# A searched instruction order for two mixer-and-MLP layers on one core: 857 of its 1187 operations reordered

## The chip, the cores and the metric

The kernel runs on one NeuronCore of one Trainium2 chip. The core has five engines with instruction queues of their own: TensorE (PE in the profile; its weight loads are PEld), VectorE (DVE), ScalarE (ACT), GpSimd (POOL) and SyncE (SP), which here issues nearly all the DMAs. The metric is device time in microseconds (us) of one execution; the kernel before took 236.13 us, the median of three runs (235.84 to 236.35).

## The reference

The input q is a sequence of 2048 tokens with 512 channels. Four residual steps follow each other, a mixer A and an MLP B, twice:

```python
x = A_q
x = x + _A_ref(_layernorm(x), A_k, A_v, A_shift_k, A_ssm_k, A_ssm_D)
x = x + _B_ref(_layernorm(x), B_w1, B_b1, B_w2, B_b2)
x = x + _A_ref(_layernorm(x), A_k, A_v, A_shift_k, A_ssm_k, A_ssm_D)
x = x + _B_ref(_layernorm(x), B_w1, B_b1, B_w2, B_b2)
```

A shifts k through a four-tap filter, multiplies it by v, convolves the product along the sequence with a kernel as long as the sequence (`ssm_k`, by FFT in the reference, plus `ssm_D` times the product), and multiplies the result by the normalised x. Since the convolution does not depend on x, its output Y is computed once and used in both layers. B normalises again, multiplies by w1 (512 x 1376), adds b1, takes a gelu, multiplies by w2 (1376 x 512) and adds b2.

## The kernel before

The program records 1187 operations with `P.op`, each with the engines that may run it, a duration used for planning, and what it reads and writes. An operation is one instruction, or a group of matmuls on one accumulator. `arrange` then places them: `SEQ` is a list of operation numbers that gives the global order (each engine's queue is that list cut to its own operations, and runs strictly in it), `ENGS` gives the engine of each operation that could run on more than one, and `BANKS` the PSUM bank of each accumulator. `sync` adds the semaphore waits that the order needs. All three tables were written by a search outside the kernel.

The first part of the program, roughly to 55 us of the span, computes the convolution of the first 1024 tokens as a Fourier transform made of matmuls: `ht`, `h1`, `h2` (transform of the filter), `fir` (the shift and the product with v), `x1`, `x2` (transform of the product), elementwise products, and `i1`, `i2` (inverse). The second 1024 tokens go through the same stages (`h2_1`, `fir4` to `fir7`, `x1_1`, `x2_1`, `i1_1`, `i2_1`) between the MLP work of the first half. Three of their steps use DMAs from one part of the on-chip memory to another or from DRAM: eight `swap` DMAs (L460, `ar<-ar`) exchange even and odd partitions of the filter's transform once `h2_1` (VectorE, L788) is done, and the products `p2` (VectorE, L475 on 128x2048) multiply what they bring; eight transposing loads of k (L800) fill the shift's input.

The layers are worked in 13 blocks of tokens, numbered 0 to 12: of 128 or 256 tokens in the first half (L920's matmuls have 128 or 256 columns there), of 512 in the second. Block n goes through: `q` statistics (VectorE L831, L832; then L836, L838, L846 or L843 on GpSimd or VectorE), the normalisation (ScalarE L856 or VectorE L857), `y` (two products or sums on VectorE, L475), `z` statistics and normalisation the same way, a transposition of the normalised 128x512 tile so that channels lie on partitions, then `m1` (PE L920, eleven groups of four matmuls, each followed by a gelu on ScalarE, L925), `m2` (PE L954, eleven matmuls per 128 tokens) and the residual sum (VectorE L958). The transposition is done by PE in blocks 0 and 1, and by a DMA transpose (L900, issued by SP) in blocks 2 to 12: two or four of them per block, 30 in all. The first matmul group of a block's `m1` needs all its transposes landed. The chain from one layer's `m2` to the next block's `m1` is long, and PE works on other blocks in that time; which, is what the tables decide.

In arrange's planning a DMA lands 2300 ns plus its bytes over 385 per ns after its issue, which is 2640 ns for one DMA transpose of 128 KB.

Of the kernel before, what the change touches and what calls it, by code (L numbers as in the profile page):

```python
# [36 lines left out]
class Prog:  # L37
# [65 lines left out]
            "vpvvvvavvavvvvvavavpvvvaa")  # L103
    BANKS = (
            "26624320240260660466027405640260464422140204626240406006442460424046462002242440224402622420604066466004"
            "64437020665061071760610567714342477554774645676076415011601640607710627426534031026021423236345773476356"
            "05721367332244501304047053300705405345357130760457666515312732321600130735714203533")

    def __init__(self, nc):
# [885 lines left out]
```

## Time and profile before

| what | value |
| --- | --- |
| median of 3 runs (range) | 236.13 us (235.84 to 236.35) |
| the profiled execution's own time | 238.78 us |
| its span, first to last instruction | 237.0 us |
| PE busy | 224.1 us (95%) |
| VectorE busy | 179.1 us (76%) |
| ScalarE busy | 165.8 us (70%) |
| GpSimd busy | 50.0 us (21%) |
| granted TensorE clock | 1.0 throughout |

The profiled execution is 2.65 us longer than the median of the runs. A row of the waits names the waiting engine and line, then who ended the wait. A row of the chain says what the end of the program hung on at that time, in order of time. A row of the timeline gives start, duration, engine, line, and output and input tiles: `ar` is the on-chip array that holds nearly everything in bf16, `sm` the small statistics in fp32, `ps` the PSUM. SPq is SP issuing a DMA, which takes SP's time too; the DMA's landing comes later.

### The profile page before, as it was taken

What the parts mean: (1) busy time and instruction counts of PE and PEld (TensorE: products, weight loads), DVE (VectorE), ACT (ScalarE), POOL (GpSimd) and SP (SyncE); (2) the same over time, 40 slices, a digit from 0 to 9 for tenths busy, and PEclk for the clock granted to TensorE, in tenths of its full rate; (3) what the DMA queues carried; (4) which work ended last, traced back from release to release, by engine and by line L of the source; (5) the groups of instructions that cost most, each with busy time, mean ns of one, the idle gap of its engine ahead of it and who ended that gap; (6) DMA issues with size and microseconds to landing.
All of it is one profiled execution on the core that took longest, in us unless ns stands there. A gap on an engine that the chain in (4) does not pass through costs nothing.

```text
span 237.0 us, 6515 instructions
## 1 busy us (share of the span) xinstructions
PE 224.1 (95%) x2765; PEld 146.0 (62%) x2765; DVE 179.1 (76%) x363; ACT 165.8 (70%) x263; POOL 50.0 (21%) x110
## 2 busy tenths in 40 slices
PE   6888887999989979999999999999999999999995
PEld 3777776967848577667967575744444444444444
DVE  0698999999999899689999987584459779414013
ACT  3788999999948669998997999677047305731730
POOL 2270122007402453244002431303020110200000
PEclk9999999999999999999999999999999999999999
DMA  6999489938949520032500203400400140142002
GB/s 192 375 386 278 155 248 265 313 80 124 181 111 284 98 24 0 4 45 46 173 9 3 47 3 66 111 3 19 116 0 3 22 111 0 22 69 110 23 21 70
DMA packets 40105, 24.93 MB, mean 105 GB/s; under 512 B 23590, under 2 KB 33676, under 8 KB 40076
## 3 DMA queue, kind: packets, MB, share of 16 engines
q1 hardware_dynamic: 39778, 24.36, 38.6%
q8 instruction: 22, 0.36, 0.6%
q10 hardware_dynamic: 298, 0.16, 0.3%
q14 instruction: 7, 0.06, 0.1%
HBM read 13.23 MB, written 2.10 MB: 65 GB/s over the span
## 4 chain that ended last, share of the span: by engine, by line
PE 75%; ACT 8%; DMA 8%; DVE 5%; SPq 1%; issue 1%
PE ps L920 32%; PE ps L954 28%; DMA ar<-ar 6%; ACT ar L480 6%; PE ps L695 4%; PE ps L590 3%; PE ps L578 3%; DMA ar<-in_A_ssm_k_dram 2%; ACT ar L856 2%; DVE ar L475 2%; DVE ar L641 2%; PE ps L717 1%; DVE ar L481 1%; PE ps L635 1%; SPq L460 1%
## 5 line engine op out<-in xcount | busy, mean ns | idle before, releaser
L925 ACT ACTIVATE ar<-ps,sm 128x256 bf16<-128x256 f32 (+4 forms) x143 | 66.1, 521 | 37.2 <-PE ps L920 36.8
L920 PE MATMUL ps<-ar 128*128 128x256 bf16 (+4 forms) x572 | 81.6, 297 | 2.9 <-DMA ar<-ar 2.7
L480 ACT ACTIVATE ar<-ps 128x1024 bf16<-128x1024 f32 (+3 forms) x78 | 72.1, 1003 | 12.1 <-PE ps L578 4.8
L954 PE MATMUL ps<-ar 128*128 128x512 bf16 (+1 forms) x341 | 79.6, 379 | 0.0
L920 PEld LDWEIGHTS ps<-ar 128*128 128x128 bf16 (+1 forms) x572 | 52.6, 100 | 30.2 <-DMA ar<-ar 3.7
L475 DVE TENSOR_TENSOR ar<-ar 128x512 bf16<-128x512 bf16 (+2 forms) x104 | 62.9, 642 | 5.9 <-ACT ar L856 4.4
L954 PEld LDWEIGHTS ps<-ar 128*128 128x128 bf16 (+1 forms) x341 | 32.3, 98 | 35.1 <-ACT ar L925 0.2
L831 DVE BATCH_NORM_STATS2 sm<-ar 128x6 f32<-128x512 bf16 x64 | 42.8, 683 | 0.5
L958 DVE TENSOR_TENSOR ar<-ar,ps 128x512 bf16<-128x512 bf16 x31 | 20.8, 680 | 28.7 <-PE ps L954 28.7
L856 ACT ACTIVATE ar<-ar,sm 128x512 bf16<-128x512 bf16 x39 | 30.7, 811 | 10.2 <-DVE sm L843 10.2
L838 POOL TENSOR_TENSOR sm<-sm 128x2 f32<-128x2 f32 (+2 forms) x26 | 21.4, 824 | 41.4 <-DVE sm L836 39.8
L836 POOL TENSOR_SCALAR sm<-sm 128x2 f32<-128x2 f32 (+2 forms) x19 | 5.9, 310 | 92.0 <-DVE sm L832 91.8
L590 PE MATMUL ps<-ar 128*128 128x64 bf16 x512 | 18.5, 193 | 1.7 <-DVE ar L481 0.6
L578 PE MATMUL ps<-ar 128*64 128x128 bf16 x512 | 18.3, 221 | 1.9 <-ACT ar L480 1.2
L590 PEld LDWEIGHTS ps<-ar 128*128 128x128 bf16 x512 | 16.9, 98 | 4.7 <-DVE ar L481 1.2
L578 PEld LDWEIGHTS ps<-ar 128*64 128x64 bf16 x512 | 15.0, 110 | 5.0 <-ACT ar L480 2.6
L481 DVE CAST ar<-ps 128x1024 bf16<-128x1024 f32 x11 | 13.4, 1216 | 1.5 <-PE ps L578 1.2
L846 POOL TENSOR_SCALAR sm<-sm 128x1 f32<-128x1 f32 x34 | 13.6, 414 | 1.7
L695 PE MATMUL ps<-ar 64*128 64x64 bf16 (+1 forms) x384 | 12.4, 203 | 0.6 <-DVE ar L475 0.4
L695 PEld LDWEIGHTS ps<-ar 64*128 64x128 bf16 (+1 forms) x384 | 11.8, 113 | 1.8 <-ACT ar L480 0.7
L857 DVE TENSOR_SCALAR ar<-ar,sm 128x512 bf16<-128x512 bf16 x25 | 9.8, 413 | 2.5 <-POOL sm L846 2.2
L832 DVE BATCH_NORM_AGGREGATE sm<-sm 128x2 f32<-128x6 f32 x64 | 10.5, 173 | 0.8
(45 smaller groups left out, 93.1 us busy)
## 6 DMA issues: line engine op xcount, KB each, us to landing
ar<-ar SPq DMA_DIRECT2D x16, 256.0 KB, 3.6
ar<-tab_s SPq DMA_DIRECT2D x9, 256.0 KB, 6.4
ar<-in_A_ssm_k_dram SPq DMA_DIRECT2D x8, 256.0 KB, 5.8
ar<-in_A_q_dram SPq DMA_DIRECT2D x8, 256.0 KB, 5.1
ar<-in_A_v_dram SPq DMA_DIRECT2D x8, 256.0 KB, 5.2
out_dram<-ar SPq DMA_DIRECT2D x7, 256.0 KB, 2.5
ar<-in_B_w_dram SPq DMA_DIRECT2D x4, 344.0 KB, 4.6
ar<-in_B_w_dram SPq DMA_DIRECT2D x5, 256.0 KB, 5.2
```

Source lines behind the costliest of these rows:

```text
L475: return P.op(eng, lambda e: e.tensor_tensor(o, a, b, op), dur, reads=[a, b] + list(more), writes=[o])
L480: return e.activation(dst, src(), AF.Copy)
L578: r = e.matmul(Q(tl, 64 * ri, 64, i * 128, [1, 128]), w, m, start=True, stop=True)
L590: r = e.matmul(Q(tl, 0, 128, i // 8 * 512 + i % 8 * 4, [32, 16], [1, 4]), w, m, start=True, stop=True)
L695: r = e.matmul(Q(tl, 0, 128, i, *([32, 16], [1, 4]) if split else ([1, 128],)), w, m, start=n == 0, stop=n == 1)
L831: P.op(DVE, lambda e, sj=sj, x=x: e.bn_stats(sj, x), 600.0, reads=[x], writes=[sj])
L838: P.op(POOL, lambda e: e.tensor_tensor(r, v, hf, ALU.pow), 420.0 + 149.0 * n, reads=[v, hf], writes=[r])
L856: return e.activation(o, x, AF.Identity, bias=u, scale=r)
L920: r = e.matmul(Q(tl, 0, rows, 0, [1, w]), a, m, start=dk == 0, stop=dk == 3)
L925: P.op(ACT, lambda e, dst=dst, tl=tl, rows=rows, bias=bias, w=w: e.activation(dst, Q(tl, 0, rows, 0, [1, w]), AF.Gelu_apprx_tanh, bias=bia ...
L954: r = e.matmul(Q(tl, 0, 128, 0, [1, 512]), ins[fc][0], ins[fc][1], start=fc == 0, stop=fc == 10)
L958: P.op(DVE, lambda e, x=x, tl=tl: e.tensor_tensor(x, x, Q(tl, 0, 128, 0, [1, 512]), ALU.add), 604.0, reads=[x], writes=[x], tile=tl)
```

## The change

The first 330 numbers of `SEQ` stay. The 857 others stand in a new order, found by a search like the one before in which each on-chip DMA transpose had a longer time reserved than the 2640 ns. With the new order, 25 operations run on another engine of those allowed (nine move from ScalarE to VectorE, eight the other way, five from VectorE to GpSimd, three back), and most accumulators of the reordered part are in other banks. The operations themselves, their sizes and the code around the tables are the same, and so are the durations in `arrange`. The first line that differs in `SEQ`, cut:

```diff
-        419, 414, 258, 411, 389, 412, 415, 293, 456, 588, 413, 416, 482, 408, 417, 251, 460, 409, 534, 452, 461, 426,
...
+        419, 414, 482, 411, 389, 448, 415, 258, 292, 456, 449, 466, 534, 457, 454, 483, 467, 412, 486, 455, 452, 588,
...
```

What moves is seen on the engines' queues. On VectorE, around block 2's second statistics: L788 is `h2_1` of the convolution, L475 on 128x512 is `y` of blocks 2 and 3, L831 and L832 are the `z` statistics of block 2. Before:

```order
L788 SCALAR_TENSOR_TENSOR ar<-ar,sm,ps 128x16x32 x6
L475 TENSOR_TENSOR ar<-ar 128x512
L788 SCALAR_TENSOR_TENSOR ar<-ar,sm,ps 128x16x32
L475 TENSOR_TENSOR ar<-ar 128x512
L788 SCALAR_TENSOR_TENSOR ar<-ar,sm,ps 128x16x32
L831 BN_STATS sm<-ar 128x6
L475 TENSOR_TENSOR ar<-ar 128x512
L832 BN_AGGR sm<-sm 128x2
L831 BN_STATS sm<-ar 128x6
L832 BN_AGGR sm<-sm 128x2
L788 SCALAR_TENSOR_TENSOR ar<-ar,sm,ps 128x16x32 x5
```

And now:

```order
L788 SCALAR_TENSOR_TENSOR ar<-ar,sm,ps 128x16x32 x5
L475 TENSOR_TENSOR ar<-ar 128x512
L788 SCALAR_TENSOR_TENSOR ar<-ar,sm,ps 128x16x32
L475 TENSOR_TENSOR ar<-ar 128x512 x2
L831 BN_STATS sm<-ar 128x6 x2
L832 BN_AGGR sm<-sm 128x2 x2
L788 SCALAR_TENSOR_TENSOR ar<-ar,sm,ps 128x16x32 x2
L843 SCALAR_TENSOR_TENSOR sm<-sm 128x2
```

Ahead of block 2's statistics there were eight L788 and now there are six; L843, the negated mean, was on GpSimd (as L846) and is now on VectorE behind two more L788.

On ScalarE, around block 3's second normalisation: the rows of 128x256 and 96x256 are the eleven gelus of block 2; the first two L856 among or behind them normalise block 3's two tiles for their DMA transposes, the next ones are block 4's, and L480 empties an accumulator of `x1_1`. Before:

```order
L925 ACTIVATE ar<-ps,sm 128x256 x7
L925 ACTIVATE ar<-ps,sm 96x256
L925 ACTIVATE ar<-ps,sm 128x256
L856 ACTIVATE ar<-ar,sm 128x512
L925 ACTIVATE ar<-ps,sm 128x256 x2
L856 ACTIVATE ar<-ar,sm 128x512 x2
L480 ACTIVATE ar<-ps 128x1024
L856 ACTIVATE ar<-ar,sm 128x512
```

And now:

```order
L925 ACTIVATE ar<-ps,sm 96x256
L925 ACTIVATE ar<-ps,sm 128x256 x7
L856 ACTIVATE ar<-ar,sm 128x512
L925 ACTIVATE ar<-ps,sm 128x256
L856 ACTIVATE ar<-ar,sm 128x512
L925 ACTIVATE ar<-ps,sm 128x256 x2
L856 ACTIVATE ar<-ar,sm 128x512 x2
L480 ACTIVATE ar<-ps 128x1024
```

The first of the two moved ahead of one gelu, the second ahead of two, and the second of block 4 ahead of the L480.

On SP, in the same place, the queue of DMAs before (L800 loads k, L900 are the DMA transposes of blocks 2 and on, the eight L460 of `ar<-ar` the swaps):

```order
L800 DMA_TRANSPOSE ar<-in_A_k_dram 128x4x128
L900 DMA_TRANSPOSE ar<-ar 128x4x128 x2
L460 DMA ar<-ar 64x8x256 x8
L900 DMA_TRANSPOSE ar<-ar 128x4x128 x8
L460 DMA ar<-in_A_q_dram 128x1024 x4
```

And now:

```order
L900 DMA_TRANSPOSE ar<-ar 128x4x128 x2
L460 DMA ar<-ar 64x8x256 x5
L900 DMA_TRANSPOSE ar<-ar 128x4x128 x4
L460 DMA ar<-ar 64x8x256 x3
L900 DMA_TRANSPOSE ar<-ar 128x4x128 x4
L460 DMA ar<-in_A_q_dram 128x1024 x4
```

Three of the eight swaps now stand behind the four transposes of blocks 3 and 4.

On ScalarE in the stage of `x2_1`: L480 with 128x2x16x32 empties an accumulator of `x2_1`, L925 are gelus of blocks 4 and 5, L856 normalises block 6. Before:

```order
L480 ACTIVATE ar<-ps 128x2x16x32
L856 ACTIVATE ar<-ar,sm 128x512 x2
L480 ACTIVATE ar<-ps 128x2x16x32 x3
L925 ACTIVATE ar<-ps,sm 128x256
L480 ACTIVATE ar<-ps 128x2x16x32 x2
L925 ACTIVATE ar<-ps,sm 128x256
L925 ACTIVATE ar<-ps,sm 96x256
L925 ACTIVATE ar<-ps,sm 128x256 x2
L480 ACTIVATE ar<-ps 128x2x16x32
L925 ACTIVATE ar<-ps,sm 128x256 x11
```

And now:

```order
L480 ACTIVATE ar<-ps 128x2x16x32
L856 ACTIVATE ar<-ar,sm 128x512 x2
L925 ACTIVATE ar<-ps,sm 96x256
L480 ACTIVATE ar<-ps 128x2x16x32 x4
L925 ACTIVATE ar<-ps,sm 128x256 x3
L480 ACTIVATE ar<-ps 128x2x16x32
L925 ACTIVATE ar<-ps,sm 128x256 x15
```

The longest run of these evacuations was three and is now four; the gelus that stood between them now stand before or after.

More of the change, by code (lines that the diff above doesn't have):

```diff
@@ L58 @@
         533, 445, 424, 260, 209, 410, 422, 425, 586, 286, 446, 261, 423, 587, 406, 447, 294, 418, 257, 250, 407, 388,
[41 rows of a table removed]
[41 rows of a table added]
     ENGS = (
             "pvavvvvvavpvpapapaaavaaaaavaavaavavvvppvvvaavvaaavaavvaaaaaaaaavaaaaavaaaavaaaaaaapppvaaaaaaaaaaaaaaaaaa"
-            "aaaaaaaaaaapvapvvavpvppaappvvppaavpaappaappaappaappaappaappavppaappaavpvvppavppaapvaavavvvaaapvvavvvpaav"
-            "vpvvvvavvavvvvvavavpvvvaa")
+            "avaaaaaaaaapvapvvavpvppaappvvpvaavpaappaappaappaappaappavppvappaappaappvappaapvaapvavvavvvvvapvvvvvppvaa"
+            "avvvvaappavvapvavavpvvava")
     BANKS = (
-            "26624320240260660466027405640260464422140204626240406006442460424046462002242440224402622420604066466004"
-            "64437020665061071760610567714342477554774645676076415011601640607710627426534031026021423236345773476356"
-            "05721367332244501304047053300705405345357130760457666515312732321600130735714203533")
+            "26624320240260660466027405640260464422140204626240406006442460424046462022442640460444626002206020640220"
+            "04023022660051677767117660640311026376367637332542537030213654742352762454741476061377362300423726574027"
+            "07315704314621527766215047034261015330227471565340011503350731745320154030276054756")
     def __init__(self, nc):
```

80 rows, old and new, of the table SEQ are left out of this document.

## The prediction

> **What bounds the kernel now.** I read the page's busy times first, then the busy time by stage, then the waits, and last the chain around the waits that PE has. In the table by stage each row gives a stretch, its length, and each engine's busy time in it.
>
> ```profile
> span 237.0 us, 6515 instructions
> PE 224.1 (95%) x2765; PEld 146.0 (62%) x2765; DVE 179.1 (76%) x363; ACT 165.8 (70%) x263; POOL 50.0 (21%) x110
> ...
> 44.00:56.00 12.00, 11.62 (x197) 9.03 (x194) 11.60 (x28) 11.13 (x14) 2.02 (x5) 1.00 0.63 147
> 56.00:71.20 15.20, 13.91 (x286) 10.51 (x284) 15.17 (x31) 11.63 (x31) 5.38 (x14) 1.00 0.72 144
> 71.20:84.30 13.10, 11.49 (x171) 7.87 (x172) 12.41 (x27) 8.52 (x16) 4.18 (x12) 1.00 0.75 175
> 84.30:125.00 40.70, 40.70 (x479) 29.90 (x479) 37.69 (x54) 37.61 (x68) 11.61 (x16) 1.00 0.18 43
> 125.00:153.00 28.00, 27.89 (x404) 18.79 (x404) 24.03 (x68) 24.33 (x38) 9.11 (x18) 1.00 0.22 49
> 153.00:235.00 82.00, 81.54 (x403) 38.58 (x400) 43.57 (x105) 36.20 (x59) 6.40 (x11) 1.00 0.17 41
> ```
>
> PE is the bound. From 84.3 us to 235 us it is busy 150.1 of 150.7 us, and the change alters no matmul: nothing can be won there, only lost. The first 330 operations are kept, which covers the first 44 us. What is left to win lies between 44 and 84.3 us, where PE misses 0.38 + 1.29 + 1.61 = 3.3 us. VectorE misses only 0.40 + 0.03 + 0.69 = 1.1 us there, so it is close behind.
>
> The waits name who ended PE's idle time, with the total, the number of waits and the longest:
>
> ```profile
> PEld ps L920 <- DMA ar<-ar: 3.7, 2, 2.1
> PE ps L920 <- DMA ar<-ar: 2.7, 2, 1.6
> ```
>
> Two waits of `m1` for a DMA transpose hold 2.7 of the 3.3 us. The chain shows both:
>
> ```profile
> 66.84 4.29 DMA ar<-ar
> 71.14 0.05 issue
> 71.19 4.55 PE ps L920 x40
> ...
> 77.67 0.71 ACT ar L856
> 78.38 0.49 SPq L900
> 78.87 0.45 issue
> 79.31 4.88 DMA ar<-ar
> 84.20 0.05 issue
> 84.25 7.60 PE ps L920 x68
> ```
>
> The first is block 2's second transpose: issued at 66.84, landed 4.29 us later. The second is block 3's, which also found SP still busy with the issue before it: its normalisation ended at 78.38, its issue came at 79.31. The timeline gives PE's own wait in each place, in the brackets:
>
> ```profile
> 71.19 4.98 PE L920 MATMUL ps<-ar 128*128 128x256 bf16 x44 [1.06 <-DMA ar<-ar]
> 84.25 1.92 PE L920 MATMUL ps<-ar 128*128 128x256 bf16 x16 [1.61 <-DMA ar<-ar]
> ```
>
> All 30 transposes together took this long to land (least, median, most), and a stretch without other traffic shows what one takes alone:
>
> ```profile
> DMA to landing us min/median/max: 2.4/2.5/4.9
> ...
> ar<-ar SPq DMA_TRANSPOSE x4, 2.5
> ```
>
> So the two that PE waited for, at 4.29 and 4.88 us, were late by 1.8 and 2.4 us against 2.5. The DMA table of the stretch 66.8 to 71.2 has one packet of the instruction queue beside the swaps, and so has 79.3 to 84.3; the undisturbed stretch (186 to 195 us, block 11) has none.
>
> ```profile
> q8 instruction: 1, 0.02, 1.6%
> ...
> q8 instruction: 1, 0.02, 1.1%
> ...
> q8 instruction: 22, 0.36, 0.6%
> ```
>
> [...]
>
> **The change part by part.**
>
> *Block 2's transposes.* Two L788 fewer stand on VectorE ahead of block 2's statistics, and VectorE is never idle there (15.17 of 15.20 us), so the statistics, the normalisations and the transposes behind them come earlier by those two instructions:
>
> ```profile
> 57.52 1.40 DVE L788 SCALAR_TENSOR_TENSOR ar<-ar,sm,ps 128x512 bf16<-128x512 bf16 x2
> ```
>
> That is 1.40 us, more than the 1.06 us wait. PE's work between the same points is the same set of groups in another order. The wait closes even if the transpose is as late as it was: -1.06 us. If only the ordinary 2.5 us is needed, the result is the same.
>
> *Block 3's transposes.* The second normalisation now stands ahead of two gelus that stood before it:
>
> ```profile
> 76.84 0.83 ACT L925 ACTIVATE ar<-ps,sm 128x256 bf16<-128x256 f32 x2
> ...
> 68.16 7.13 SPq L460 DMA_DIRECT2D ar<-ar  x8
> 76.96 4.01 SPq L900 DMA_TRANSPOSE ar<-ar  x2
> ```
>
> It comes 0.83 us earlier. In the trace eight swaps occupied SP from 68.16 to 75.29, and SP needed 4.01 us for the two issues (half of 2.50 each where nothing disturbs, in a row below), so the second was issued 0.93 us (79.31 less 78.38) after it was ready. With five swaps ahead, the DMA queue has about 3/8 x 7.13 = 2.7 us more to drain. The bounds are 0.83 us won (SP stays as slow) and the whole 1.61. I take the middle, -1.22 us.
>
> *Blocks 0 and 1, 54 to 66 us.* The groups of `m1` of both blocks are mixed anew and PE follows the gelus closely; PE misses 0.38 us in 44 to 56 and 1.29 - 1.06 = 0.23 us in 56 to 71.2 apart from the transpose. I take half a repeat of the 0.23 on top, 0.12 us; the bounds are -0.2 (they vanish) and +0.5 (as much again as 0.38 + 0.12).
>
> *The three swaps behind block 4.* They were all issued by 75.29 us, and now wait in SP's queue for block 4's second normalisation, which ended at 82.78 in the trace:
>
> ```profile
> 81.98 0.80 ACT L856 ACTIVATE ar<-ar,sm 128x512 bf16<-128x512 bf16 x1
> ...
> 85.37 1.19 DVE L475 TENSOR_TENSOR ar<-ar 128x2048 bf16<-128x2048 bf16 x1
> ...
> ar<-ar SPq DMA_DIRECT2D x16, 256.0 KB, 3.6
> ...
> L831 DVE BATCH_NORM_STATS2 sm<-ar 128x6 f32<-128x512 bf16 x64 | 42.8, 683 | 0.5
> L475 DVE TENSOR_TENSOR ar<-ar 128x2048 bf16<-128x2048 bf16 x24 | 28.1, 1215 | 0.2 <-ACT ar L480 0.2
> L475 DVE TENSOR_TENSOR ar<-ar 128x512 bf16<-128x512 bf16 x64 | 25.4, 417 | 5.3 <-ACT ar L856 4.4 <-ACT ar L480 0.5
> ```
>
> One more issue of 1.25 us and two of 0.89 us (7.13 / 8) later, at about 85.8, the last swap is issued; with 3.6 us it lands at 89.4, and at 91.8 if late by 2.4. Its first user is the fifth `p2`. The second one started at 85.37; from there the new order has three `p2`, three L831 and four L475 of 128x512 ahead of the fifth, 3 x 1.215 + 3 x 0.683 + 4 x 0.417 = 7.4 us, so it is due at 92.7. That covers the late case as well: nothing.
>
> *The other blocks, 84 us on.* The nine operations that go to VectorE and the eight that come back leave its load as it was. PE's 0.6 us of idle time in 150.7 is not to be bettered, so the reordering can only cost here, by small waits or by a late transpose. The 18 transposes from 107 to 191 us all landed in 2.4 to 2.5 us. Block 7 shows the room that they have:
>
> ```profile
> 132.11 2.50 SPq L900 DMA_TRANSPOSE ar<-ar  x2
> ...
> 137.33 0.93 PE L920 MATMUL ps<-ar 128*128 128x256 bf16 x7
> ...
> DMA to landing us min/median/max: 2.4/2.5/2.5
> ```
>
> The second was issued near 133.4, so it had 3.9 us, and one as late as 4.88 would cost 1.0 us. I take one such meeting in four programs, +0.25 us; the bounds are 0 and 2.0 (two meetings in one program).
>
> *The sum.* -1.06 - 1.22 + 0.12 + 0.25 = -1.91 us. Against the profiled execution it is 238.78 - 1.91 = 236.9 us. The median of the runs is 2.65 us shorter than that execution; taking the same off the median gives 236.13 - 1.91 = 234.2 us. The best that the bounds allow is -1.06 - 1.61 - 0.2 = -2.87, 233.3 us; the worst is -1.06 - 0.83 + 0.5 + 2.0 = +0.6, 236.7 us.
>
> **The rivals.**
>
> *The waits belong to the profiled execution.* The profiled execution is 2.65 us longer than the median, and the two waits make 1.06 + 1.61 = 2.67 us. If the runs without profile have no late transposes, there is nothing to win: 236.13 + 0.12 + 0.25 = 236.5 us, or 236.25 without a late transpose elsewhere. [...] In this case the new order is the same or a little slower.
>
> *VectorE takes over.* It misses only 1.1 us between 44 and 84.3, and its work is the same. If PE, freed of 2.3 us, is then held by VectorE, whose products and sums release banks and tiles, at most 1.1 us remain: 236.13 - 1.1 = 235.0 us. Against it speaks that VectorE idles 3.0 us in the next stage, so it may lag and catch up. That is faster too.
>
> *Slower: ScalarE falls behind in the stage of `x2_1`.* From 84.3 to 125 us ScalarE is busy 37.61 of 40.70 us, and PE never waits for it. That is a property of the old order. The new one puts four evacuations of `x2_1` in a row on ScalarE where at most three stood, with gelus of blocks 4 and 5 behind them:
>
> ```profile
> L480 ACT ACTIVATE ar<-ps 128x1024 bf16<-128x1024 f32 (+3 forms) x78 | 72.1, 1003 | 12.1 <-PE ps L578 4.8
> ```
>
> Each such evacuation takes 1.0 us, and a gelu of 0.4 us that stands one evacuation later frees its PSUM bank and its part of `m2`'s input 1.0 us later. PE waits for that only if its own order has nothing else in between. The rival decides from about 1.9 us of PE waits between 84 and 153 us, two evacuations' worth, on; with three it is 236.13 - 1.91 + 3.0 = 237.2 us. For it speaks that three engines run at over nine tenths in that stage, so that a lateness is not made good soon; against it, that the same amount of work fitted without a single wait before.
>
> **How the numbers follow.** The forecast gets 0.42 (234.2 us), the profile-only rival 0.27 (half of it within 0.2%, half slower), the VectorE bound 0.10 (235.0, faster), the late ScalarE or a like loss on PE 0.21 (237.2, slower). A change of 0.2%, 0.47 us, is about what a measurement of this kernel can tell from none. That gives faster 0.42 + 0.10 = 0.52, same 0.27 x 0.5 = 0.14, slower 0.13 + 0.21 = 0.34. The range reaches from the best of the bounds, 233.3, past the worst of them and over the last rival to 237.4 us; the likeliest case's own range is 233.3 to 235.6, the upper end being the edge of what can be told from no change.
>
> **What the profile of the changed kernel would show.** Right: PE's waits of L920 for a DMA fall from 2.7 to under 0.5 us, block 2's and block 3's `m1` begin with no wait, and the stage after 84 us stays filled to over 99%. The three swaps land before VectorE's fifth `p2`. Wrong: a new row of PE waiting for a DMA at a later block (a late transpose with too little room); VectorE waiting for a DMA near 90 us (late swaps); PE waiting for ScalarE from 55 to 66 us, or from 95 to 125. If the waits are gone from the profile, its execution is some 2 us shorter and the runs are not, then the waits belonged to the profile.

## The result and the profile after

The changed kernel takes 236.12 us (median of 22 runs, 235.63 to 237.01). The kernel before, run beside it on the same chip, takes 237.16 us (median of 22 runs, 235.84 to 240.13). The ratio is 0.9968, 95% interval 0.9953 to 0.9983: 0.32% faster, where 0.8% was forecast, and 1.9 us above the forecast time. Later batches gave ratios of 0.9954, 0.9954 and 0.9970 (their intervals are in the table of the experiments). The three runs of the kernel before that the prediction had (235.84, 236.13, 236.35) were low ones: over five batches on several chips its runs look like this beside those of the changed kernel over four.

| kernel | runs | lowest | lower quartile | median | upper quartile | highest | at or below 236.5 us | above 237 us |
| --- | --- | --- | --- | --- | --- | --- | --- | --- |
| before | 146 | 235.49 | 236.41 | 237.00 | 237.58 | 240.13 | 41 | 72 |
| changed | 58 | 235.63 | 235.93 | 236.14 | 236.31 | 237.09 | 51 | 3 |

The fastest runs of both are nearly the same. What the change took away is the upper part of the spread. All three runs that the prediction started from lie in the lowest quarter of the old kernel's.

The profiled execution took 235.91 us, against 238.78. From its page, the span and the busy times:

```profile
span 234.0 us, 6498 instructions
PE 222.7 (95%) x2743; PEld 147.1 (63%) x2765; DVE 178.7 (76%) x362; ACT 164.5 (70%) x262; POOL 55.5 (24%) x113
```

The busy time by stage, with the stages cut at the same events as before (PE starts block 2's `m1` at 70.44 us and block 3's at 81.86 now, at 71.19 and 84.25 before; the cut at 81.7 is 0.16 us early):

```profile
56.00:70.40 14.40, 14.06 (x289) 10.73 (x286) 14.09 (x28) 11.82 (x31) 4.98 (x13) 1.00 0.98 184
70.40:81.70 11.30, 11.09 (x184) 7.76 (x170) 11.30 (x27) 8.75 (x16) 4.09 (x10) 1.00 0.39 96
81.70:122.40 40.70, 40.17 (x528) 30.77 (x533) 40.12 (x59) 37.08 (x68) 16.50 (x18) 1.00 0.26 63
```

The two stages that held the waits are 0.8 and 1.8 us shorter as cut (1.64 us for the second from start to start, 11.42 for 13.06), and PE fills them but for 0.34 and 0.21 us. (22 of PE's 2765 matmul records are missing in this profile, so its busy time is a little higher than shown.) All that PE waits for from 44 to 150 us:

```profile
PE ps L954 <- issue: 0.6, 4, 0.2
PE ps L717 <- ACT ar L480: 0.3, 1, 0.3
PE ps L908 <- ACT ar L480: 0.3, 1, 0.3
PE ps L920 <- ACT ar L480: 0.2, 1, 0.2
PE ps L954 <- DVE ar L475: 0.2, 1, 0.2
```

The row of L920 waiting for a DMA, 2.7 us before, is gone. Both `m1` start with no bracket behind them, which means no idle time ahead:

```profile
70.44 3.26 PE L920 MATMUL ps<-ar 128*96 128x256 bf16 x28
...
81.86 2.35 PE L920 MATMUL ps<-ar 128*128 128x256 bf16 x20
```

The transposes were not all prompt, though. The 30 together (least, median, most):

```profile
DMA to landing us min/median/max: 2.4/2.5/4.2
```

By a refill is meant from here on one packet of the queue named `instruction` (q8 in the DMA tables; 22 packets and 0.36 MB in the whole execution, before and after). The late transposes were block 4's (4.11 and 3.34 us), block 5's (3.31) and block 12's (4.18 and 3.33), each with a refill in flight, and block 2's first (3.50 us), without one. Nothing waited for any of them: block 4's landed at 84.08 and is used at 86.56, block 2's landed by 68.25 and are used at 70.44.

### The profile page after: what moved, and what is told of

Its sections match the earlier page's. It is cut to its first block, busy times and chain, and to the rows that moved or that the text cites. A ratio compares the mean times of both kernels' runs of the same rounds, so it can differ in the third digit from the quotient of the medians.

```text
span 234.0 us, 6498 instructions
## 1 busy us (share of the span) xinstructions
PE 222.7 (95%) x2743; PEld 147.1 (63%) x2765; DVE 178.7 (76%) x362; ACT 164.5 (70%) x262; POOL 55.5 (24%) x113
## 4 chain that ended last, share of the span: by engine, by line
PE 58%; DVE 24%; ACT 10%; issue 2%; POOL 2%; DMA 2%; SPq 0%; DVEq 0%
PE ps L920 23%; PE ps L954 23%; DVE ar L475 13%; ACT ar L480 9%; PE ps L695 4%; DVE sm L831 3%; PE ps L590 2%; DMA ar<-in_A_ssm_k_dram 2%; DVE ar L672 2%; DVE ar L958 2%; DVE ar L641 2%; PE ps L717 1%; POOL sm L836 1%; PE ps L578 1%; PE ps L635 1%
## 5 line engine op out<-in xcount | busy, mean ns | idle before, releaser
L925 ACT ACTIVATE ar<-ps,sm 128x256 bf16<-128x256 f32 (+5 forms) x143 | 65.7, 523 | 33.2 <-PE ps L920 32.9
L920 PE MATMUL ps<-ar 128*128 128x256 bf16 (+5 forms) x569 | 81.9, 297 | 0.4 <-ACT ar L480 0.2
L480 ACT ACTIVATE ar<-ps 128x1024 bf16<-128x1024 f32 (+3 forms) x77 | 71.1, 998 | 11.0 <-PE ps L578 3.4
L954 PE MATMUL ps<-ar 128*128 128x512 bf16 (+1 forms) x323 | 75.9, 379 | 1.5 <-issue 0.6
L920 PEld LDWEIGHTS ps<-ar 128*128 128x128 bf16 (+1 forms) x572 | 52.9, 100 | 27.5 <-ACT ar L480 1.1
L475 DVE TENSOR_TENSOR ar<-ar 128x512 bf16<-128x512 bf16 (+2 forms) x104 | 62.7, 646 | 1.5 <-ACT ar L480 0.8
L831 DVE BATCH_NORM_STATS2 sm<-ar 128x6 f32<-128x512 bf16 x64 | 42.5, 685 | 0.5
L856 ACT ACTIVATE ar<-ar,sm 128x512 bf16<-128x512 bf16 x39 | 30.6, 813 | 12.9 <-DVE sm L843 8.8
L836 POOL TENSOR_SCALAR sm<-sm 128x2 f32<-128x2 f32 (+2 forms) x22 | 9.9, 449 | 89.0 <-DVE sm L832 88.8
L838 POOL TENSOR_TENSOR sm<-sm 128x2 f32<-128x2 f32 (+2 forms) x26 | 21.7, 834 | 25.1 <-DVE sm L836 23.1
L481 DVE CAST ar<-ps 128x1024 bf16<-128x1024 f32 x12 | 14.6, 1218 | 1.2 <-PE ps L578 0.9
L846 POOL TENSOR_SCALAR sm<-sm 128x1 f32<-128x1 f32 x34 | 15.1, 460 | 1.6
L695 PE MATMUL ps<-ar 64*128 64x64 bf16 (+1 forms) x384 | 12.4, 203 | 1.0 <-DVE ar L475 0.9
L695 PEld LDWEIGHTS ps<-ar 64*128 64x128 bf16 (+1 forms) x384 | 11.8, 113 | 2.2 <-DVE ar L475 1.0
L857 DVE TENSOR_SCALAR ar<-ar,sm 128x512 bf16<-128x512 bf16 x25 | 10.3, 415 | 2.7 <-POOL sm L846 2.5
L788 DVE SCALAR_TENSOR_TENSOR ar<-ar,sm,ps 128x512 bf16<-128x512 bf16 x16 | 11.1, 740 | 0.3 <-PE ps L590 0.3
```

The lines of the kernel that those rows point to most:

```text
L475: return P.op(eng, lambda e: e.tensor_tensor(o, a, b, op), dur, reads=[a, b] + list(more), writes=[o])
L480: return e.activation(dst, src(), AF.Copy)
L695: r = e.matmul(Q(tl, 0, 128, i, *([32, 16], [1, 4]) if split else ([1, 128],)), w, m, start=n == 0, stop=n == 1)
L831: P.op(DVE, lambda e, sj=sj, x=x: e.bn_stats(sj, x), 600.0, reads=[x], writes=[sj])
L838: P.op(POOL, lambda e: e.tensor_tensor(r, v, hf, ALU.pow), 420.0 + 149.0 * n, reads=[v, hf], writes=[r])
L856: return e.activation(o, x, AF.Identity, bias=u, scale=r)
```

## The experiments

What was open: whether the wait for late transposes is a matter of single executions or of the order; what makes a transpose late; and which part of the new order gives the gain. Each kernel is compared with the kernel before on the same chip. The times are medians; kernels of one batch ran on one chip, beside the same runs of the kernel before.

| kernel | batch | time (range), us | runs | ratio (95% interval) | profiled span, us | of it PE waiting for a block's transpose |
| --- | --- | --- | --- | --- | --- | --- |
| before (first profile) | | | | | 237.0 | 2.7 |
| before again | 1 | 237.22 (236.28 to 238.05) | 10 | 1.0022 (0.9999 to 1.0046) | 235.4 | 1.0 |
| before, block 3's norms earlier | 1 | 237.33 (236.53 to 237.89) | 10 | 1.0024 (1.0001 to 1.0048) | 235.6 | 1.2 |
| before, refills shifted | 1 | 237.06 (236.45 to 237.98) | 10 | 1.0021 (1.0002 to 1.0041) | 235.6 | 0 |
| changed, refills shifted | 1 | 236.91 (236.59 to 237.66) | 10 | 1.0020 (0.9997 to 1.0043) | 234.9 | 0 |
| before again | 2 | 236.90 (235.92 to 237.88) | 12 | 0.9991 (0.9962 to 1.0019) | 234.4 | 0 |
| changed again | 2 | 236.18 (235.66 to 237.03) | 12 | 0.9954 (0.9928 to 0.9980) | 234.2 | 0 |
| before, blocks 2 and 3 earlier | 2 | 236.54 (236.14 to 237.61) | 12 | 0.9985 (0.9962 to 1.0007) | 234.8 | 0 |
| changed, a statistic of block 5 moved | 2 | 236.12 (235.74 to 236.83) | 12 | 0.9966 (0.9946 to 0.9985) | 233.9 | 0 |
| changed, block 2 later | 3 | 237.61 (237.05 to 237.98) | 12 | 1.0023 (1.0005 to 1.0042) | 235.6 | 1.3 |
| changed, swaps ahead again | 3 | 236.23 (235.72 to 236.85, and one of 328.91) | 12 | 0.9955 (0.9936 to 0.9973) | 234.7 | 0 |
| before, block 2 earlier | 3 | 236.20 (235.85 to 238.26) | 12 | 0.9965 (0.9944 to 0.9986) | 234.2 | 0 |
| changed again | 3 | 236.16 (235.84 to 237.09) | 12 | 0.9954 (0.9932 to 0.9977) | 234.6 | 0 |
| changed, a statistic of block 6 moved | 4 | 236.15 (235.95 to 236.78) | 12 | 0.9976 (0.9959 to 0.9993) | 234.9 | 0 |
| changed again | 4 | 235.97 (235.64 to 236.81) | 12 | 0.9970 (0.9952 to 0.9987) | 233.8 | 0 |

The kernel before gave 1.0022 and 0.9991 against itself, so a single ratio is good to about 0.2%. Between 1.7 and 2.0 us lie around the span in every run.

**The kernel before, again (twice).** No edit.

> The kernel before, unchanged, for a second profile. Theory 1 (meetings): PE's two waits for a DMA transpose (1.06 us at block 2, 1.61 at block 3 in the profile of before) come about when a refill packet of the instruction queue meets the transpose, and differ from execution to execution; a second profile has another sum of these waits, between 0 and 2.7 us, and its span is 234.3 us (237.0 less 2.67) plus that sum, within 0.3. Theory 2 (fixed contention with the swaps): both waits are there again at about their size, and the span is near 237 us.

> The kernel before, unchanged, run beside the others on one chip. Theory (a transpose is late only when an instruction refill meets it): its time is 236 to 238 us with a ratio to itself of 0.998 to 1.002, and its profiled execution has a span of 234.3 us plus TensorE's waits of L920 for a DMA, within 0.4 us; by the four profiles of this order so far 0 to 2.7 us of such waits, most likely about 1.0 us, all of it at block 2 and sometimes block 3. Rival (the order itself sets the wait, and every execution has the same one): the wait is the same 1.0 us at block 2 as in the last profile of this order, and the runs lie within 0.3 us of each other.

The first of these profiles shows one wait, at block 2; the timeline has it in the bracket, and block 3 starts with none:

```profile
71.35 2.36 PE L920 MATMUL ps<-ar 128*128 128x256 bf16 x20 [1.05 <-DMA ar<-ar]
...
82.64 3.55 PE L920 MATMUL ps<-ar 128*128 128x256 bf16 x31
```

The second has no wait at all:

```profile
70.36 3.33 PE L920 MATMUL ps<-ar 128*128 128x256 bf16 x29
...
81.64 4.53 PE L920 MATMUL ps<-ar 128*128 128x256 bf16 x40
```

So the same program waits 2.7, 1.0 or 0 us, and its span less the wait is 234.3, 234.4 and 234.4 us. The DMA table of block 2's transposes tells why. In the first, from 67.0 to 71.3 us, one packet of the instruction queue is among the transfers, and the transpose takes 4.3 us:

```profile
q8 instruction: 1, 0.02, 1.6%
...
ar<-ar SPq DMA_TRANSPOSE x1, 4.3
```

In the second, from 67.0 to 69.5, there is none, and both take 2.5:

```profile
q1 hardware_dynamic: 1088, 0.26, 52.0%
issues: line engine op xcount, KB each, median us to landing
ar<-ar SPq DMA_DIRECT2D x2, 256.0 KB, 4.4
ar<-ar SPq DMA_TRANSPOSE x2, 2.5
```

The refill came at 69.14 us in the first, 2.1 us after the transpose's issue at 67.02. In the second it came at 69.62, 2.4 us after the issue at 67.24, when the transpose was 0.13 us from landing. Here half a microsecond of scatter decided. The rival, that the order has the same wait in every execution, fell. A transpose that has no room waits or not by chance, and the spread of the runs agrees with that.

Without such a wait the two orders take nearly the same time. PE reaches L695 in the part that both share; its row in the second of these profiles, and in the profile after:

```profile
41.55 3.65 PE L695 MATMUL ps<-ar 128*128 128x128 bf16 x62 [0.55 <-DVE ar L475]
...
41.32 3.86 PE L695 MATMUL ps<-ar 128*128 128x128 bf16 x65 [0.90 <-DVE ar L475]
```

From there to the end of the span it is 192.8 us in the old order and 192.7 in the new one (234.4 - 41.55 and 234.0 - 41.32). The three repeats of the new order give 192.7 too. So the new order gains some 0.1 us apart from the waits.

**Block 3 alone.** The kernel before, with block 3's two z norms one gelu and two gelus earlier on ScalarE (rows of the queue; L925 are block 2's gelus, L856 the norms):

```diff
 L925 ACTIVATE ar<-ps,sm 96x256
+L856 ACTIVATE ar<-ar,sm 128x512
 L925 ACTIVATE ar<-ps,sm 128x256
 L856 ACTIVATE ar<-ar,sm 128x512
 L925 ACTIVATE ar<-ps,sm 128x256 x2
-L856 ACTIVATE ar<-ar,sm 128x512 x2
+L856 ACTIVATE ar<-ar,sm 128x512
```

> The kernel before with one part of the change alone: block 3's first normalisation ahead of one gelu and its second ahead of two (ScalarE), nothing else moved. Both theories of the transposes: block 3's wait is closed or falls by about 0.8 us, block 2's stays as it may be; 0.2 to 0.8 us faster than before in the median (ratio 0.9965 to 0.999). Theory 3 (the gain lies elsewhere in the new order): no change, ratio 1.000.

It gave nothing, though both theories had 0.2 to 0.8 us: 1.0024, where the unchanged kernel had 1.0022 in the same batch. Its profile shows why (the edit makes lines 5 higher, so L925 is L920 here). Block 3's first transpose met a refill, took 4.56 us and still landed at 81.42, ahead of PE at 82.87. What PE waited for was block 2's, 4.43 us with a refill at 69.02:

```profile
71.58 1.59 PE L925 MATMUL ps<-ar 128*128 128x256 bf16 x13 [1.20 <-DMA ar<-ar]
...
82.87 1.36 PE L925 MATMUL ps<-ar 128*128 128x256 bf16 x11
```

**The refills shifted, in both orders.** The program starts with a warm-up, seven matmuls on zeros of 512 columns. Splitting them into 71 of 50 columns puts 64 more matmuls, each with its weight load (128 instructions), at the head of PE's queue, with nearly the same number of columns (3550 for 3584). That the refills then come earlier in the program was the author's supposition.

```diff
-        for i in range(7):
-            r = e.matmul(Q(tl, 0, 128, 0, [1, 512]), z[:, :128], z, start=True, stop=True)
+        for i in range(71):
+            r = e.matmul(Q(tl, 0, 128, 0, [1, 50]), z[:, :128], z[:, :50], start=True, stop=True)
```

> [...] The warm-up writes nothing that is read. Theory 1: the refills fall some 64 weight loads earlier in the program, so they meet other transposes; block 2's and 3's waits change, and the median moves by 0.5 to 2 us in one or the other direction. Theory 2: the waits are as in before and the ratio is 1.000 within 0.002.

> The changed kernel with the same split of the warm-up. Theory 1: its rooms of about 4.9 us at blocks 2 and 3 cover a meeting, so it stays at the changed kernel's ratio to before, 0.997 within 0.002, unless a refill meets a transpose of a later block with 3.5 to 4 us of room, which would show as one new wait of up to 1 us. Theory 2: the same, 0.997, with no new wait.

The refills did move, though by how many weight loads is not shown: in the old order they came at 66.6, 72.1 and 81.3 us, where its first profile had them at 62.6, 68.9, 77.6 and 82.1. The one at 66.6 ended 0.5 us after block 2's first transpose was issued (67.26), and none began while block 2's transposes were in flight. The DMA table from 66.7 to 69.7 us, which counts the packets that begin there, has none of the instruction queue, and both took 2.5 us:

```profile
q1 hardware_dynamic: 557, 0.13, 22.0%
issues: line engine op xcount, KB each, median us to landing
ar<-ar SPq DMA_TRANSPOSE x2, 2.5
```

PE had no wait for them. Those of block 6 (4.08 us) and block 10 (4.05) were late instead, which had been prompt in every profile without the shift; those of block 12, late in every one of these, were prompt. So the late transposes go with the refills, not with the blocks. In the new order a refill at 65.9 us met block 2's first transpose (3.19 us), and PE did not wait for it. The times missed both expectations: theory 1 had 0.997 for the new order and a move of 0.5 to 2 us for the old one, and both came out at 1.002. The edit has a price of its own: without a wait for a transpose the shifted kernels have spans of 235.6 and 234.9 us, their unshifted twins 234.4 and 233.8 to 234.6. Most of it lies in the part that both orders share: PE reaches L695 (here L700) at 42.81 and 42.32 us, against 41.16 to 41.90 in the unedited kernels. But with no wait for block 2 in either profile the two orders differ by 0.15 us (237.06 and 236.91), against 0.7 to 1.1 us in the four batches without the shift, and the old order's runs scatter with a standard deviation of 0.40 us, against 0.74 for the kernel before and 0.57 for its repeat in the same batch.

**The changed kernel, again.** No edit.

> The changed kernel, unchanged, beside the kernel before on the same chip. Theory (the longer reserve covers the refills): the ratio is 0.996 to 0.998 (0.5 to 1.0 us faster), the profiled execution shows no wait of L920 for a DMA above 0.3 us though some transposes take over 3 us, and its runs spread less than those of the kernel before. Rival (the gain measured at first was the chip's scatter): the ratio is 0.999 to 1.001.

> The changed kernel once more, as the yardstick for the two edits of it on the same chip. All theories: 0.4 to 1.1 us faster than the kernel before, its runs within 1.5 us of each other, its profiled execution 234.0 us in span within 0.3 us, without a wait of L920 for a DMA.

Both as the theory said, the gain (0.9954) just past the upper edge of what was expected, and the second span, 234.6 us, 0.3 past it. The standard deviation of the twelve runs is 0.33 and 0.34 us (kernel before in these batches: 0.78 and 0.68), and no profile has a wait of L920 for a DMA, though the longest transpose took 3.9 and 4.3 us.

**Room for blocks 2 and 3, in the old order.** Block 3's edit is the one above. For block 2 its two z norms and a gelu go ahead of two q norms, and its negated mean from GpSimd to VectorE:

```diff
 L925 ACTIVATE ar<-ps,sm 128x128 x2
-L856 ACTIVATE ar<-ar,sm 128x512 x3
+L856 ACTIVATE ar<-ar,sm 128x512 x2
+L925 ACTIVATE ar<-ps,sm 128x128 x2
+L856 ACTIVATE ar<-ar,sm 128x512 x2
 L925 ACTIVATE ar<-ps,sm 128x128
 L856 ACTIVATE ar<-ar,sm 128x512
-L925 ACTIVATE ar<-ps,sm 128x128
-L856 ACTIVATE ar<-ar,sm 128x512
-L925 ACTIVATE ar<-ps,sm 128x128
```

> The order before with one thing of the new one alone: block 2's z norms and one gelu stand ahead of two q norms on ScalarE, block 2's negated mean is on VectorE, and block 3's z norms stand ahead of three gelus, so that the transposes of both blocks start 0.4 to 0.9 us earlier against their first use. Everything else is as before. Theory (room at blocks 2 and 3 is where the gain comes from): it is 0.4 to 0.8 us faster than before, ratio 0.9965 to 0.9985, and the profile's wait of L920 for a DMA is 0.6 us or less. Rival (the gain comes from the whole of the new order, the stages behind 84 us with it): ratio 0.999 to 1.002, as with block 3's norms alone (1.0024).

0.9985 lies at the edge of what the theory gave, and its interval takes in 1: by itself this run decides nothing. The wait is gone, the runs spread less (standard deviation 0.40 us), but the span without a wait is 234.8 us.

**Room for block 2 alone, in the old order.** The last diff without block 3's part.

> The order before with block 2's part of the earlier edit alone: block 2's z norms and one gelu ahead of two q norms, and its negated mean on VectorE, block 3 as before. Theory (block 2 is nearly always met by the refill, block 3 sometimes): most of the 0.6 us that both parts together gave, so 0.3 to 0.6 us faster than before, with single runs up to 1.6 us slower than the fastest, from block 3. Rival (both parts are needed): within 0.1% of the kernel before.

0.9965: nearly the whole gain, from two norms, a gelu and one small statistic. Eleven of its twelve runs lie from 235.85 to 236.54 us and one at 238.26, so something can still be late, as the expectation had it for block 3; that run has no profile. The profiled one has no wait:

```profile
70.16 3.55 PE L920 MATMUL ps<-ar 128*128 128x256 bf16 x31
...
81.44 4.75 PE L920 MATMUL ps<-ar 128*128 128x256 bf16 x42
```

From the one to the other it takes 11.28 us, as in the undisturbed execution of the old order (81.64 - 70.36). With block 3's norms earlier too it took 11.57 (70.53 to 82.10) in the one profile, 0.3 us more. That this is the price of block 3's part is not shown: with that part alone it took 11.29 (71.58 to 82.87), behind a late block 2. The medians of 236.54 and 236.20 us come from two chips, and the intervals of their ratios overlap.

**Room taken away, in the new order.** Block 2's second z norm stands behind the last q norm of the stage:

```diff
-L925 ACTIVATE ar<-ps,sm 128x128
-L856 ACTIVATE ar<-ar,sm 128x512
+L925 ACTIVATE ar<-ps,sm 128x128 x2
+L856 ACTIVATE ar<-ar,sm 128x512 x2
 L925 ACTIVATE ar<-ps,sm 128x128
 L856 ACTIVATE ar<-ar,sm 128x512 x2
-L925 ACTIVATE ar<-ps,sm 128x128
-L856 ACTIVATE ar<-ar,sm 128x512
```

> The changed kernel with one thing undone: block 2's second normalisation on ScalarE stands two q norms of block 4, a gelu and a q norm of block 3 later, so that its DMA transpose, issued at 65.5 us in the profile after, is issued at about 68.1 us. Its first use, block 2's m1, is at 70.4 us. Theory (block 2's room is what the new order won): the transpose lands at 70.6 us at the earliest, TensorE waits 0.1 to 0.4 us for it in most executions and about 2 us in those where a refill comes early enough to meet it (the refill came at 70.2 to 70.4 in the three profiles of this order); 0.2 to 1.2 us slower than the changed kernel on the same chip, and a wider spread of its runs. Rival (the gain is spread over the new order): within 0.1% of the changed kernel.

237.61 us, 1.45 us slower than the changed kernel on the same chip, so the whole gain is lost and more. Its transpose was issued at 69.07 us, a microsecond later than expected, and landed 2.98 us later with a refill beside it:

```profile
69.07 1.79 SPq L900 DMA_TRANSPOSE ar<-ar  x1
...
72.09 1.62 PE L920 MATMUL ps<-ar 128*96 128x256 bf16 x13 [1.29 <-DMA ar<-ar]
```

The loss is a little over the expected 1.2 us, and the expected wider spread did not come (standard deviation 0.26 us). PE was ready at 70.80 us, and at 2.47 us, as without a refill, the transpose would have landed at 71.54: issued this late it would be waited for whether a refill meets it or not. Chance needs a transpose that is just in time.

**The swaps ahead again, in the new order.** SyncE's queue:

```diff
-L460 DMA ar<-ar 64x8x256 x5
-L900 DMA_TRANSPOSE ar<-ar 128x4x128 x4
-L460 DMA ar<-ar 64x8x256 x3
-L900 DMA_TRANSPOSE ar<-ar 128x4x128 x4
+L460 DMA ar<-ar 64x8x256 x8
+L900 DMA_TRANSPOSE ar<-ar 128x4x128 x8
```

> The changed kernel with one thing undone: the three swaps stand again ahead of block 3's transposes on SyncE, so that eight swaps are issued before them. The prediction's term for this was 0.4 us of SyncE's time (0 to 0.8) at block 3. Theory (the swaps hold up SyncE's issues of block 3's transposes): the second of block 3's transposes is issued 0.4 to 0.9 us later than at 76.9 us, and lands at 79.9 to 80.5 us instead of 79.5; since its first use is at 81.7 us the time changes by less than 0.1%, and by 0.5 us at most if a refill meets it. Rival (the swaps do not matter to SyncE): it is issued within 0.2 us of where it was, and nothing changes.

The time is that of the changed kernel, 0.9955 and 0.9954 (the run of 328.91 us had a granted clock of 0.66, the other eleven 1.0, and is not in the ratio). SyncE's issues of the four transposes of blocks 3 and 4, from the timeline of the changed kernel in the same batch and then from that of this edit:

```profile
75.94 7.44 SPq L900 DMA_TRANSPOSE ar<-ar  x4
```

```profile
76.16 7.65 SPq L900 DMA_TRANSPOSE ar<-ar  x4
```

Block 3's second was issued 1.65 us behind its first, against 1.31 with the swaps behind (77.81 - 76.16 and 77.25 - 75.94): 0.34 us, less than the theory's 0.4 to 0.9 and more than the rival's 0.2. A refill met the first (3.93 us), it landed at 80.09, and PE came at 82.65. Moving the swaps was worth nothing here.

**A GpSimd operation that took 3.34 us.** In the profile after, the chain runs through a small statistic on GpSimd (128x2), which takes 0.19 us in most other places. It starts with VectorE's three products of two inputs and ends with them:

```profile
90.35 3.34 POOL L836 TENSOR_SCALAR sm<-sm 128x2 f32<-128x2 f32 x1 [8.07 <-DVE sm L832]
...
90.16 3.48 DVE L475 TENSOR_TENSOR ar<-ar 128x2048 bf16<-128x2048 bf16 x3
```

The first try moved one letter of `ENGS`, so that one scaled variance (L836) runs on VectorE:

```diff
-            "avaaaaaaaaapvapvvavpvppaappvvpvaavpaappaappaappaappaappavppvappaappaappvappaapvaapvavvavvvvvapvvvvvppvaa"
+            "avaaaaaaaaapvapvvavpvppaappvvpvaavpaappaappaappaappaavpavppvappaappaappvappaapvaapvavvavvvvvapvvvvvppvaa"
```

> The changed kernel with one operation of block 5's z statistics (the scaled variance of L836, 128x2) on VectorE in place of GpSimd, where it took 3.34 us in the profile after, beside VectorE's three two-input products of 128x2048 in 3.48 us. Theory (the GpSimd operation was held up by those products, and block 5's chain with it): the operation takes under 0.3 us on VectorE, no GpSimd operation of 128x2 takes over 1.5 us at 88 to 96 us of the profile, and the time is 0 to 0.6 us below the changed kernel's on the same chip. Rival (block 5's chain has room, as PE is over 98% busy there): the ratio equals that of the changed kernel within 0.1%.

It was the wrong one: block 5's, ten microseconds later. The operation at 90.3 us took 3.34 us again, and the time is the changed kernel's (236.12 and 236.18). The second try moved the right one, block 6's, with two statistics of block 5 ahead of the products. VectorE's queue:

```diff
 L832 BN_AGGR sm<-sm 128x2
+L836 TENSOR_SCALAR sm<-sm 128x2
+L832 BN_AGGR sm<-sm 128x2
+L831 BN_STATS sm<-ar 128x6
 L475 TENSOR_TENSOR ar<-ar 128x32x64 x3
 L958 TENSOR_TENSOR ar<-ar,ps 128x512
 L475 TENSOR_TENSOR ar<-ar 128x32x64
-L832 BN_AGGR sm<-sm 128x2
-L831 BN_STATS sm<-ar 128x6
```

> The changed kernel with the GpSimd operation that took 3.34 us at 90.35 us put elsewhere. It is the scaled variance (L836) of block 6's q statistics, not of block 5's z statistics, which the run before moved by mistake. It now runs on VectorE right behind its variance, with two of VectorE's z statistics of block 5 behind it, ahead of the three products of 128x2048, so that GpSimd's next two operations (L838, L846) run beside operations with one input. Theory (GpSimd is held up while those products run): no GpSimd operation between 85 and 96 us takes over 1.2 us, and block 6's q chain ends some 2.5 us earlier; since TensorE's waits from 44 us on are only 1.6 us in the profile after, and none of them is for that chain, the time falls by 0.3 us at most, and may rise by as much, since the products come 1.3 us later. Rival (the operation is slow in itself): L838 takes over 2 us in its place.

> The changed kernel, as the yardstick for the run beside it. Faster than the kernel before by 0.4 to 1.1 us, and the GpSimd operation at 90.4 us takes 3.3 us again.

The hold-up only moved to the two GpSimd operations of L846, which began 0.31 us after the products. The row of L846 holds two of 128x1, of 2.08 and 1.25 us (0.50 us for such a pair elsewhere):

```profile
91.38 0.71 POOL L838 TENSOR_TENSOR sm<-sm 128x2 f32<-128x2 f32 x1 [8.27 <-DVE sm L836]
92.19 3.30 POOL L846 TENSOR_SCALAR sm<-sm 128x1 f32<-128x1 f32 x2
...
91.88 3.48 DVE L475 TENSOR_TENSOR ar<-ar 128x2048 bf16<-128x2048 bf16 x3
```

The operation is not slow in itself: L836 took 0.17 us on VectorE and L838 0.71 on GpSimd. The theory's bound of 1.2 us failed all the same, because 1.3 us of other work was too short a shelter. Nor is GpSimd always held up by all three products. With the swaps ahead again the same L836 began 0.17 us into the first of them (90.96 to 92.15) and ended just behind it:

```profile
91.13 1.07 POOL L836 TENSOR_SCALAR sm<-sm 128x2 f32<-128x2 f32 x1 [8.07 <-DVE sm L832]
```

In the new order with the refills shifted it took 1.08 us, in the six other profiles that have it there 3.34 or 3.35. What decides is open. The time is 236.15 against 235.97 us, which is not told apart. So the hold-up costs the kernel nothing that can be measured, and none of these versions beats the changed kernel.

## Why the prediction was wrong

The direction and the cause were right, the size was not. In the likeliest case the time was to be 234.2 us; it was 236.12. The step that failed is the last of the sum: "The median of the runs is 2.65 us shorter than that execution; taking the same off the median gives 236.13 - 1.91 = 234.2 us." The waits of 1.06 and 1.61 us were those of one execution. They can't be taken off a median of three runs that lie 2.65 us lower, because by all that the runs show those were lower by not having the waits. An undisturbed execution of the old order has a span of 234.4 us, the new one 233.8 to 234.6, so there were no 234.2 us in time, some 232.4 in span, to be had. The 1.9 us that the forecast is too low fall into two parts: the base was low by 1.03 us (237.16 in 22 runs beside the change, 236.13 in three), and the gain was 1.04 in place of 1.91, 0.87 less.

- *Block 2's transposes, -1.06 us.* Right in place, and in size for an execution that has the wait. They were issued at 64.25 and 65.48 us, the second 1.36 us earlier than before where 1.40 was forecast, and landed by 68.25, 2.2 us ahead of `m1` and of the refill at 70.3. Room at block 2 alone gave 0.9965 in the old order, and its loss cost 1.45 us in the new one.
- *Block 3's transposes, -1.22 us.* The mis-sized term. The median gains next to nothing from it. In the pair of profiles the whole 1.61 us went, but of the five profiles that have block 3's old norms only the first shows that wait; a lone edit of block 3 gave nothing. The 4.88 us behind that wait were a rare case too: the refill named for it began at 82.14, 2.83 us after the issue, when a transpose of 2.5 us would have landed. The transpose ahead of it had a refill beside it as well (77.57), and no other transpose on record landed so late. The part of this term that came from SyncE and the swaps was 0.34 us of issue and nothing of time.
- *The remix of blocks 0 and 1, +0.12 us, and late transposes elsewhere, +0.25 us.* PE's waits from 44 to 70.4 us are 0.8 us in the profile after and 0.5 in a repeat of it, all for ScalarE. From L695 to block 2's `m1` it is 29.12 us now and 28.81 in the undisturbed old order, so the remix costs 0.3 us, inside the bounds. No run shows the one costly meeting in four programs that the +0.25 us stands for: a refill met a transpose at blocks 4, 5 and 12 in all four profiles of the unedited new order, far more often than one program in four, and PE never waited. Price nil: in the profile after, block 4's landed 2.5 us ahead of its use and block 5's 3.3 us (104.49 for 107.82). That behind 84 us nothing could be won was wrong by a little: from block 3's `m1` to the end it is 152.7 us in each profile of the old order and 152.2 in the profile after. Part of that may be work moved ahead of this point, since together the new order gains only 0.1 us.
- *The swaps behind block 4, nothing.* Right: the last landed at 87.90 us, for use at 90.16.
- *VectorE takes over.* VectorE makes up most of the chain from 66 to 124 us in the profile after (24% of the span; 26%, 24% and 5% in the three repeats, 5% before), without holding PE for more than the 0.2 us of the waits' table.
- *ScalarE falls behind.* No wait of PE for ScalarE behind 84 us.
- *The waits belong to the profiled execution.* This rival had the time (236.25 to 236.5) nearly right. But the waits need no profile: the runs of the old kernel scatter up to 240.13 us without one. What the rival's near equality of 2.65 and 2.67 us said was that the profiled execution was disturbed and the three runs were not.

The packet of the instruction queue that the prediction found beside both late transposes is borne out by more than one place now. In the sixteen profiles 476 DMA transposes of the blocks can be followed to their landing. 344 had no refill packet in flight: median 2.47 us, 333 of them at most 2.6, five over 3.0. 132 had one: median 3.21 us, 81 over 3.0, the longest 4.88. What counts is when the packet begins. Where it began 0.1 to 2.1 us after the transpose's issue, all 66 took 2.91 to 4.65 us; where it began 2.2 to 2.5 us after it, the transpose was about to land and all 23 took 2.40 to 2.54. The 42 with a packet that had begun before or at the issue are mixed (2.41 to 3.78). The refills shifted moved the late ones with them. PE itself was busy 40.70 of 40.70 us from 84.3 to 125 us of the old order's first profile while three refills came (at 95.2, 103.5 and 114.3 us); the transpose issued 0.84 us ahead of the second of them took 3.91 us.

What stays open: how a packet that lasts 0.9 to 2.1 us makes a transpose up to 2.2 us late (4.65 for 2.47), what made the 4.88 us (a packet of a second instruction queue, q14, began 0.62 us after its issue), and whether the single runs above 239 us of the old kernel had both waits or something else.

## What to carry to other kernels

Before a wait seen in one profile is taken off a time, compare that execution with the runs: where it is longer than they are by just that wait, the runs' floor already lacks it, and what can be won is the distance of the median from the floor, for which three runs are too few. A DMA that lands just ahead of its use can turn a scatter of half a microsecond into one of whole microseconds (here waits of 1.06, 1.05 and 0 us for block 2 in the same program), so give it room against the latest landing that the trace shows, and only where a late one is waited for: here room for one block (a landing at 68.97 us for a use at 70.16) was worth as much as 857 operations in a new order. Room for the other block, whose wait one profile in five showed, brought no gain that these runs can tell.

## What the runs showed of the hardware

- Where a refill began 0.1 to 2.1 us after the issue of a DMA transpose from one part of the on-chip memory to another, the transpose landed late: 2.91 to 4.65 us in all 66 cases of the sixteen profiles, against a median of 2.47 without one. Where it began 2.2 to 2.5 us after the issue, the transpose took 2.40 to 2.54 us in all 23 cases.
- Another load may do it too, to a lesser degree; this is not shown. The five transposes over 3.0 us without a refill (3.22 to 3.51) are all the first of block 2 in the new order, issued at 64.1 to 65.1 us, 0.6 to 0.9 us behind a load of v, which was in flight. In three more profiles the same load was in flight too, issued 1.1 to 1.3 us ahead, and the transpose took 2.53, 2.59 and 2.87 us. In the old order that load is issued some 4 us ahead of the transposes. In the profile after, a packet of the second instruction queue (q14, 64.05 to 64.51 us) was in flight too when the 3.50 us transpose was issued, at 64.25.
- A small GpSimd operation that started beside VectorE's products of two inputs ended just behind one of them (0.05 us in the profile after and with the swaps ahead again), but not always the first of three: L836, 0.19 us in most other places, took 3.34 or 3.35 us in six profiles and 1.07 and 1.08 in two. So three such products can follow each other (3.48 us in the profile after) while GpSimd's operation is still under way. Why it is held up is not shown.
